# The expert stage of a fused attention, MLP and top-1 MoE kernel: arms in another order, part of a second layer inside them, conversions split, written order outside

## The chip, the cores and the metric

The kernel runs on one core of a Trainium2 chip (trn2). The metric is the device time of one execution in microseconds (us). TensorE does the matrix products, VectorE and ScalarE read their results and convert weights, GpSimd gathers and scatters rows by index, and SyncE (SP) issues the loads of weights.

## The reference, cut to what matters

```
attn_out = chunked attention(q, k, v, mem_k, mem_v)   # 2 x 8 heads x 768 x 64
x = tokens of attn_out                                # 1536 x 512
h = x @ w_in;  x = (h * sigmoid(1.702 * h)) @ w_out   # 512 -> 2048 -> 512
logits = x @ w_gate                                   # 8 experts
expert_idx = argmax(logits);  gate_w = its softmax probability
for each expert e: disp[e] = the tokens that chose it (at most 384)
    h = max(disp[e] @ w1[e], 0)                       # 512 -> 1024
    y = h @ w2[e]                                     # 1024 -> 512
out[token] = gate_w * y[its expert, its place]
```

The change lies in the last part, the eight experts. With the inputs that are timed, the experts get 224, 291, 128, 160, 256, 160, 189 and 128 tokens, in the order in which the kernel works them (`EORDER`). The text calls them expert 0 to expert 7 in that order.

## The kernel before, in words

All products are made in float32 from two parts: each operand is split into a high part (rounded to the matmul's type) and a low part (what is left), and three products are summed: high x high, high x low, low x high. So a weight matrix has to be converted before use. A `Piece` is a quarter of `w1` or `w2` of an expert (512 KB): `Piece.hi` (L292) writes the high part on ScalarE (L295), `Piece.lo` (L297) the low part on VectorE (L300). Each expert has eight pieces, four of `w1` and four of `w2`. They come over SP's queue (L241) into eight raw buffers; a raw buffer is free for the next load when the low part has been taken. `w_next(e, keep)` (L347) converts the next piece, both halves one behind the other, unless it is numbered `keep` or more among the pieces of expert e+1; `steps(part)` (L1027) does so until `KEEPS[part]` is reached. Six weight slots of half a matrix hold what is converted: the four of the expert at work and two more.

Tokens are worked in blocks of 128, gathered by GpSimd (L827), transposed by TensorE (`trans`, L843) and split into `xs`. Expert 0 has its first block done in the stage before and goes through `after_first` (L1162). The others go through `others` (L1186). How many blocks an expert has is known only on the chip, so `others` branches on the count in a register (`tc.If`), and each engine runs one of three arms:

- lone (at most 128 tokens; `one`, L1140, `first_of`, L1035): the first layer with the tokens as the stationary operand (`block_h`, L951, matmuls L964), its relu (L968), transposes back (`turn`, L973, L977, L978), all instructions in written order;
- narrow (129 to 192; `narrow_two`, L1144, `first_of_narrow`, L1059): eight chunks `fc` of the first layer for 192 columns (L1080, L1082, four `psh` buffers of PSUM), each read by ScalarE and VectorE into `low` (L1085, L1086) and split by `scale` (L1068, L1069), with the 64 columns of the second block packed by GpSimd into `hp` (L1071); then the second block's second layer `small2(1)` (L939);
- wide (over 192; `wide_two`, L1149, `first_of_two`, L1047): eight chunks for 256 columns (L879, L882, L883), the second layer of block 1 (L1004), and a nested branch for a third block (`third`, L1130).

In every arm w_next is called at some chunks (`PUMPS`, `PUMPS1`), the next expert's two blocks are transposed (`next_trans`, L1022), and `steps(0)` ends what the arm may convert: `KEEPS[0] = 4`, that is all four pieces of the next `w1`. Behind the arms the engines meet again (the join): the slots of `w1` are freed, the first block's whole second layer follows (`layer2_part(0, ...)`, L998, L1004: eight chunks of three matmuls), `steps(1)` converts the next `w2`, a second branch sends the second block (`send_second`: VectorE's L945 and L946 for a narrow one, ScalarE's L1009 for a wide one), and block 0 is sent.

The Tile framework puts instructions of one level in an order of its own by priority and readiness, unless dependencies are added by hand. `in_order` (L140) adds them along each engine; `turned` (L1043) does so for ScalarE and VectorE alone. Outside the arms nothing fixes the order of TensorE, ScalarE and VectorE. The pieces are counted at build time, so every arm has to convert the same pieces (`both`, L1097).

Of the kernel before, what the change touches and what calls it, by code (L numbers as in the profile page):

```python
# [21 lines left out]
P = 128  # L22
# [10 lines left out]
FROM = 150  # L33
EV1 = 2
PUMPS = (1, 3, 5)
PUMPS_N = (1, 3, 5)
RAWS = 4
RT = (4, 7)
LOADS = 1000
AHEAD = 4  # L40
EARLY = 12
KEEP = 4
KEEPS = (4, 8, 8)
HALF = P // 2
PUMPS1 = (0, 1, 1, 0)
GFC = 2
EORDER = (1, 2, 0, 3, 5, 6, 7, 4)
KNOWN = 8
TFC = 5
STEPS = (2, 4, 2, 5, 4)  # L50
TAIL1 = 8
DEPTH = 2
# [40 lines left out]
def kernel(  # L93
# [45 lines left out]
    @contextmanager  # L139
    def in_order(only=None):  # L140

        traced = nc.cur_bb.bb.instructions
        n0 = len(traced)
        yield
        last = {}
        for i in traced[n0:]:
            if only is not None and i.engine not in only:
                continue
            if i.engine in last:
                tc.add_manual_dep(  # L150
                    i, last[i.engine], mybir.DependencyInfo(mybir.DependencyClass.NoSync, mybir.DependencyReason.DATA),
                    reason="in_order")
            last[i.engine] = i.name


    const = ctx.enter_context(tc.tile_pool(name="const", bufs=1, side="left"))
    wp = ctx.enter_context(tc.tile_pool(name="wp", bufs=1, side="left"))
# [189 lines left out]
    def w_next(e, keep=KEEP):  # L347

        name, i = (flight[0].name, flight[0].i) if flight else pieces[min(w_at[0], w_end[0] - 1)][:2]
        if not flight or name[1] * 8 + 4 * (name[0] == "w2") + 2 * name[2] + i >= 8 * e + 8 + keep:  # L350
            return False
        w_step()
        w_loads(8 * F // 512)
        return True

    def w_state():
        return w_at[0], list(flight), list(free_slots), list(free_raw), dict(where), set(ready)
# [9 lines left out]
    def w_loads(n):  # L367
        while len(flight) < n and w_load():
            pass
# [446 lines left out]
    def expert_parts(e, ep, tp, cnt):  # L816
# [205 lines left out]
        def next_trans():  # L1022
            if e + 1 < E:
                parts[e + 1].trans(0)
                parts[e + 1].trans(1)

        def steps(part):  # L1027
            while w_next(e, KEEPS[part]):
                pass
# [5 lines left out]
        def first_of(b):  # L1035

            with in_order():
                turn = block_h(b, pump_one)
                next_trans()
                turn()  # L1040
                steps(0)

        def turned():  # L1043

            return in_order(only=(mybir.EngineType.Activation, mybir.EngineType.DVE))

        def first_of_two():  # L1047

            with turned():
                for fc in range(F2):  # L1050
                    mm, act = layer1(fc)
                    if fc in PUMPS:
                        w_next(e, KEEPS[0])
                    if fc == TFC:
                        with tc.issue_after(mm):
                            next_trans()
                steps(0)

        def first_of_narrow():  # L1059

            t, _ = xs_of(0)
            h = hT_of(0)
            n = P + HALF
            lows = {}

            def scale(fc):
                low = lows.pop(fc)
                nc.scalar.activation(out=h[:, 0, fc, :n], in_=low, func=AF.Relu)  # L1068
                nc.vector.scalar_tensor_tensor(out=h[:, 1, fc, :n], in0=low, scalar=0.0, in1=h[:, 0, fc, :n].bitcast(F32),  # L1069
                                               op0=ALU.max, op1=ALU.subtract)  # L1070
                nc.gpsimd.tensor_copy(hT["pair"][:, fc], h[:, :, fc, P:n])  # L1071

            with turned():
                for fc in range(F2):
                    w_tile(("w1", e, fc // 4), 0)
                    w = w_tile(("w1", e, fc // 4), 1)
                    f0 = (fc % 4) * P
                    ps = psum("h", "psh")
                    for c in range(KC):
                        nc.tensor.matmul(ps[:, :2 * n].rearrange("p (z n) -> p z n", z=2), lhsT=w[:, 0, c, f0:f0 + P],  # L1080
                                         rhs=t[:, :, c, :n], start=c == 0, stop=False)
                        mm = nc.tensor.matmul(ps[:, :2 * P], lhsT=w[:, 1, c, f0:f0 + P], rhs=t[:, 0, c, :],  # L1082
                                              start=False, stop=c == KC - 1)
                    low = lows[fc] = ep.tile([P, 512], F32, tag="hs", name="low", bufs=2)[:, :n]
                    nc.scalar.activation(out=low, in_=ps[:, n:2 * n], func=AF.Copy)  # L1085
                    nc.vector.tensor_tensor(out=low, in0=ps[:, :n], in1=low, op=ALU.add)  # L1086
                    if fc > 0:
                        scale(fc - 1)
                    if fc in PUMPS_N:
                        w_next(e, KEEPS[0])  # L1090
                    if fc == TFC:
                        with tc.issue_after(mm.ins):
                            next_trans()
                scale(F2 - 1)
                steps(0)

        def both(cond, yes, no):  # L1097

# [38 lines left out]
            with tc.If(cnt[ex] > b * P):  # L1137
                both(cnt[ex] > b * P + HALF, lambda: go(True), lambda: go(False))

        def one():  # L1140

            first_of(0)

        def narrow_two():  # L1144

            first_of_narrow()
            small2(1)

        def wide_two():  # L1149

            first_of_two()
            layer2_part(1, y_of(1), range(F2))
            third(2)

        def send_second(wide):
# [30 lines left out]
        def others():  # L1186

            assert NCB == 3
            for b in range(2):
                y_of(b)  # L1190
                gate(b)
            for b in range(2, NCB):
                load(b)
                hT_of(b)
                xs_of(b)
            both(cnt[ex] < P + 1, one, lambda: both(cnt[ex] < P + HALF + 1, narrow_two, wide_two))
            w1_done()
            layer2_part(0, y_of(0), range(F2))
            with turned():
                steps(1)  # L1200
            with tc.If(cnt[ex] > P):
                both(cnt[ex] > P + HALF, lambda: send_second(True), lambda: send_second(False))
            send(0)

        return SimpleNamespace(adopt=adopt, load=load, trans=trans, xs_of=xs_of, after_first=after_first, others=others,
# [195 lines left out]
    with ExitStack() as st:  # L1401
# [23 lines left out]
        with tc.high_priority(offset=LOADS):  # L1425
            w_loads(8 * (F // 512))
        not_before.clear()
        for e in range(E):
            if e + 1 < E:
                for b in range(2):  # L1430
                    parts[e + 1].load(b)
                parts[e + 1].xs_of(0)
            if e == 0:
                with tc.high_priority(offset=LOADS):
                    w_loads(8 * (F // 512))
                first_block.send()
                nc.gpsimd.tensor_tensor(out=pair, in0=ident[:, :HALF], in1=ident[:, HALF:], op=ALU.add)
                parts[0].after_first()
            else:
                parts[e].before_arms()  # L1440
                with tc.high_priority(offset=LOADS):
                    w_loads(8 * (F // 512))
                parts[e].others()
            for j in range(F // 512):
                w_free(("w2", e, j))


# [68 lines left out]
```

## Time and profile before

| what | us |
|---|---|
| median of three runs | 556.79 |
| lowest, highest | 552.14, 556.85 |
| profiled execution | 552.85 |
| its span, first to last instruction | 551.0 |

The profiled execution's own time is 552.85 us, of which 551.0 us is the span that the profile shows. Times in rows are microseconds from the span's start; "ns" stands for the mean of one instruction in a group. In the timeline a row is: start, length, engine, line, operation, output <- input, shape, count, and in brackets the idle time of the engine just before it and what ended it. PEld is TensorE's weight load. [...]

### The profile page before, as it was taken

Reading aid. Unit: us, or ns where it says so; the run is one execution under the profiler, and the core shown is the slowest. Engines: PE = TensorE matmul, PEld = TensorE weight load, DVE = VectorE, ACT = ScalarE, POOL = GpSimd, SP = SyncE. Lnnn points to the kernel's source line nnn. Section 1 sums busy time; section 2 is a strip of 40 time slices with the busy share of each in tenths; the row PEclk is TensorE's granted clock in tenths of the full one; section 3 lists DMA queues with packets and bytes.
Section 4 is the critical chain, followed back from the end, with each engine's and each line's share of the span. In section 5 each row is a group of like instructions: output and inputs, shape, how many; then the busy total and the mean of one; then the engine's idle time right before and its main releaser. Section 6 shows DMA issues by size and latency. Waiting matters only on the chain. (4 is left out here: it accounts for less than half of the span.)

```text
span 551.0 us, 10686 instructions
## 1 busy us (share of the span) xinstructions
PE 511.2 (93%) x4081; PEld 435.7 (79%) x4085; DVE 317.8 (58%) x637; ACT 277.8 (50%) x577; POOL 124.7 (23%) x131
## 2 busy tenths in 40 slices
PE   8799999999999999999999999999969689979674
PEld 3589889899999999999888887788849488949453
DVE  4999893678952742232474446384484838484710
ACT  2898977756642532222553344574293636455520
POOL 3335433334200120000000001530344322222200
PEclk9999999999999999999999999999999999979797
DMA  8887563142430031000484114993489566653100
GB/s 325 290 315 272 198 212 104 34 146 95 157 106 1 2 113 40 1 1 0 132 269 137 40 59 122 319 348 114 163 278 339 155 218 196 233 172 133 28 26 20
DMA packets 39158, 81.48 MB, mean 148 GB/s; under 512 B 3945, under 2 KB 10089, under 8 KB 39082
## 3 DMA queue, kind: packets, MB, share of 16 engines
q1 hardware_dynamic: 36010, 70.66, 37.8%
q0 software_dynamic: 3072, 9.80, 5.6%
q8 instruction: 48, 0.79, 0.6%
q14 instruction: 28, 0.23, 0.2%
HBM read 70.96 MB, written 9.75 MB: 146 GB/s over the span
## 5 line engine op out<-in xcount | busy, mean ns | idle before, releaser
L547 PEld LDWEIGHTS psh<-xT,w 128*128 128x128 f32 x1152 | 147.0, 188 | 7.9 <-ACT g L566 0.3
L590 PE MATMUL acc<-w,g 128*128 128x512 f32 x576 | 153.0, 400 | 0.0
L547 PE MATMUL psh<-xT,w 128*128 128x256 f32 x1152 | 151.6, 280 | 0.0
L590 PEld LDWEIGHTS acc<-w,g 128*128 128x128 f32 x576 | 100.7, 188 | 19.5 <-issue 2.1
L562 ACT ACTIVATE sg<-psh 128x256 f32<-128x256 f32 x96 | 36.7, 383 | 126.0 <-PE psh L547 125.6
L300 DVE TENSOR_TENSOR w<-raw,w 128x1024 fp32r<-128x1024 f32 x64 | 76.0, 1221 | 21.6 <-ACT w L295 15.5
L570 DVE TENSOR_TENSOR g<-sg,g 128x256 fp32r<-128x256 f32 x78 | 38.2, 490 | 80.3 <-ACT g L566 77.7
L1004 PE MATMUL psy<-w,hT 128*128 128x512 f32 x240 | 67.3, 439 | 16.6 <-ACT w L295 12.3
L1004 PEld LDWEIGHTS psy<-w,hT 128*128 128x128 f32 x240 | 50.2, 214 | 32.4 <-ACT w L295 14.4
L295 ACT ACTIVATE w<-raw 128x1024 fp32r<-128x1024 f32 x64 | 64.8, 1054 | 10.6 <-DMA raw<-in_w_dram 9.2
L827 POOL DMA_INDIRECT xr<-rows,taker x23 | 29.9, 1300 | 31.2 <-PE psy L1004 11.7
L566 ACT ACTIVATE g<-psh 128x256 fp32r<-128x256 f32 x96 | 36.3, 379 | 0.0
L601 DVE SCALAR_TENSOR_TENSOR x<-acc,x 128x512 f32<-128x512 f32 x36 | 24.1, 686 | 20.8 <-PE acc L590 20.8
L725 POOL DMA_INDIRECT y<-rows,taker x1 | 1.2, 1222 | 123.8 <-DVE cnt_i L732 123.8
L1080 PE MATMUL psh<-xs,w 128*128 128x384 f32 x96 | 28.5, 338 | 0.0
L1009 ACT ACTIVATE y<-psy,gt 128x512 f32<-128x512 f32 x10 | 6.7, 684 | 43.1 <-PE psy L1004 43.1
L1082 PE MATMUL psh<-xs,w 128*128 128x256 f32 x96 | 26.9, 280 | 0.0
L879 PE MATMUL psh<-xs,w 128*128 128x256 f32 x192 | 24.0, 284 | 2.5 <-issue 1.6
L300 POOL TENSOR_TENSOR w<-w,w 128x512 fp32r<-128x512 f32 x12 | 16.5, 1382 | 41.6 <-ACT w L295 41.4
L879 PEld LDWEIGHTS psh<-xs,w 128*128 128x128 f32 x192 | 23.3, 189 | 3.3 <-issue 1.8
L290 POOL TENSOR_TENSOR w<-w,rest 128x512 int32<-128x512 int32 x13 | 17.4, 1338 | 36.9 <-DVE w L276 33.5
L265 ACT ACTIVATE w<-raw 128x512 f32<-128x512 f32 x32 | 21.3, 674 | 8.7 <-DMA raw<-in_w_out_dram 6.7
(163 smaller groups left out, 671.6 us busy)
## 6 DMA issues: line engine op xcount, KB each, us to landing
raw<-in_w_dram SPq DMA_DIRECT2D x64, 512.0 KB, 4.9
raw<-in_w_out_dram SPq DMA_DIRECT2D x16, 512.0 KB, 3.6
raw<-in_w_in_dram SPq DMA_DIRECT2D x16, 512.0 KB, 6.3
vt<-in_v_dram SPq DMA_DIRECT2D x12, 512.0 KB, 5.3
kt<-in_k_dram SPq DMA_DIRECT2D x12, 368.0 KB, 5.2
qt<-in_q_dram SPq DMA_DIRECT2D x12, 256.0 KB, 5.1
out_dram<-blank SPq DMA_DIRECT2D x12, 256.0 KB, 2.6
rows<-x SPq DMA_DIRECT2D x5, 520.0 KB
```

Source lines behind the costliest of these rows:

```text
L295: nc.scalar.activation(out=w_dst(self.name, self.i, 0), in_=w, func=AF.Copy)
L300: eng.tensor_tensor(out=lo, in0=w, in1=hi.bitcast(F32), op=ALU.subtract)
L547: nc.tensor.matmul(ps, lhsT=w[:, wz, c, i * P:(i + 1) * P], rhs=xT[tb][:, xz, c, :], start=n == 0, stop=n == 3 * KC - 1)
L562: nc.scalar.activation(out=sg_t[u], in_=h_t[u], func=AF.Silu, scale=1.702)
L566: g_last[:1] = [nc.scalar.activation(out=g[:, 0], in_=h_t.pop(u), func=AF.Silu, scale=1.702).ins]
L570: lo = eng.tensor_tensor(out=g[:, 1], in0=sg_t.pop(u), in1=g[:, 0].bitcast(F32), op=ALU.subtract)
L590: nc.tensor.matmul(acc_t[tb][s], lhsT=g[:, gz, s * P:(s + 1) * P], rhs=w[:, wz, wi, :], start=i == 0 and n == 0, stop=u == last_of(k, tb) ...
L827: return nc.gpsimd.indirect_dma_start(out=t, out_offset=None, in_=rows[:, :], in_offset=bass.IndirectOffsetOnAxis(ap=taker[:, b, ex:ex + 1 ...
L879: mm = nc.tensor.matmul(ps, lhsT=w[:, wz, c, f0:f0 + P], rhs=t[:, xz, c, :], start=m == 0, stop=m == 3 * KC - 1)
L1004: nc.tensor.matmul(ps, lhsT=h[:, hz, fc, o:o + P], rhs=w[:, wz, fc % 4, :], start=fc == 0 and n == 0, stop=fc == F2 - 1 and n == 2)
L1080: nc.tensor.matmul(ps[:, :2 * n].rearrange("p (z n) -> p z n", z=2), lhsT=w[:, 0, c, f0:f0 + P], rhs=t[:, :, c, :n], start=c == 0, stop=False)
L1082: mm = nc.tensor.matmul(ps[:, :2 * P], lhsT=w[:, 1, c, f0:f0 + P], rhs=t[:, 0, c, :], start=False, stop=c == KC - 1)
```

## The change

The order of the three arms in the code becomes narrow, wide, lone (one condition is turned round). The first three chunks of the first block's second layer (`HEAD2 = 3`, nine matmuls) go into the arms (`head`, in the lone arm two before the last turn and one after it); the other five (`tail`) come behind the join, and now behind `steps(1)` and the second branch. The arms convert three pieces of the next `w1` and no longer four; `begin` does a piece's high half, and `end`, a chunk later, its low half and the next load. The transposes of the next expert move from the arms to just behind the join. `turned` fixes TensorE's order too. In the narrow arm a tile holds two `low` parts, so that four can be open. And `as_written` adds order dependencies along TensorE, ScalarE and VectorE for everything outside the arms, with a branch counted as an instruction of all three. Expert 0 keeps `first_of` and `w_next`.

```diff
@@ constants @@
-PUMPS_N = (1, 3, 5)
-KEEPS = (4, 8, 8)
+KEEPS = (3, 8, 8)
+HEAD2 = 3
-TFC = 5
@@ -153,6 +152,23 @@
             last[i.engine] = i.name
 
 
+    @contextmanager
+    def as_written():
+
+        traced = nc.cur_bb.bb.instructions
+        n0 = len(traced)
+        yield
+        engines = (mybir.EngineType.PE, mybir.EngineType.Activation, mybir.EngineType.DVE)
+        last = {}
+        for i in traced[n0:]:
+            arms = type(i).__name__ == "BassTileConditionalBlock"
+            mine = engines if arms else (i.engine,) if i.engine in engines else ()
+            for name in {last[x] for x in mine if x in last}:
+                tc.add_manual_dep(
+                    i, name, mybir.DependencyInfo(mybir.DependencyClass.NoSync, mybir.DependencyReason.DATA),
+                    reason="as_written")
+            last.update({x: i.name for x in mine})
+
     const = ctx.enter_context(tc.tile_pool(name="const", bufs=1, side="left"))
     wp = ctx.enter_context(tc.tile_pool(name="wp", bufs=1, side="left"))
     dram = ctx.enter_context(tc.tile_pool(name="dram", bufs=1, space=DRAM))
@@ -352,6 +368,23 @@
         w_step()
         w_loads(8 * F // 512)
         return True
+
+    def w_apart(e, keep=KEEP):
+
+        if not flight or not w_slot(flight[0].name):
+            return None
+        name, i = flight[0].name, flight[0].i
+        if name[1] * 8 + 4 * (name[0] == "w2") + 2 * name[2] + i >= 8 * e + 8 + keep:
+            return None
+        piece = flight.pop(0)
+        piece.hi()
+
+        def then():
+            piece.lo(nc.vector)
+            free_raw.append(piece.raw)
+            w_loads(8 * F // 512)
+
+        return then
 
     def w_state():
         return w_at[0], list(flight), list(free_slots), list(free_raw), dict(where), set(ready)
@@ -1042,19 +1075,55 @@
 
         def turned():
 
-            return in_order(only=(mybir.EngineType.Activation, mybir.EngineType.DVE))
+            return in_order(only=(mybir.EngineType.PE, mybir.EngineType.Activation, mybir.EngineType.DVE))
+
+        begun = []
+
+        def begin():
+
+            then = w_apart(e, KEEPS[0])
+            if then is not None:
+                begun.append(then)
+
+        def end():
+
+            if begun:
+                begun.pop(0)()
+
+        def head(b):
+
+            layer2_part(b, y_of(b), range(HEAD2))
+
+        def tail(b):
+
+            layer2_part(b, y_of(b), range(HEAD2, F2))
+
+        def first_of_one():
+
+            def pump(i):
+                if i < 2:
+                    begin()
+                if i > 1:
+                    end()
+
+            with in_order():
+                turn = block_h(0, pump)
+                begin()
+                layer2_part(0, y_of(0), range(HEAD2 - 1))
+                turn()
+                end()
+                layer2_part(0, y_of(0), range(HEAD2 - 1, HEAD2))
 
         def first_of_two():
 
             with turned():
                 for fc in range(F2):
-                    mm, act = layer1(fc)
+                    layer1(fc)
+                    end()
                     if fc in PUMPS:
-                        w_next(e, KEEPS[0])
-                    if fc == TFC:
-                        with tc.issue_after(mm):
-                            next_trans()
-                steps(0)
+                        begin()
+                head(0)
+                layer2_part(1, y_of(1), range(F2))
 
         def first_of_narrow():
 
@@ -1079,20 +1148,21 @@
                     for c in range(KC):
                         nc.tensor.matmul(ps[:, :2 * n].rearrange("p (z n) -> p z n", z=2), lhsT=w[:, 0, c, f0:f0 + P],
                                          rhs=t[:, :, c, :n], start=c == 0, stop=False)
-                        mm = nc.tensor.matmul(ps[:, :2 * P], lhsT=w[:, 1, c, f0:f0 + P], rhs=t[:, 0, c, :],
-                                              start=False, stop=c == KC - 1)
-                    low = lows[fc] = ep.tile([P, 512], F32, tag="hs", name="low", bufs=2)[:, :n]
+                        nc.tensor.matmul(ps[:, :2 * P], lhsT=w[:, 1, c, f0:f0 + P], rhs=t[:, 0, c, :],
+                                         start=False, stop=c == KC - 1)
+                    if fc % 2 == 0:
+                        two = ep.tile([P, 512], F32, tag="hs", name="low", bufs=2)
+                    low = lows[fc] = two[:, fc % 2 * 2 * P:][:, :n]
                     nc.scalar.activation(out=low, in_=ps[:, n:2 * n], func=AF.Copy)
                     nc.vector.tensor_tensor(out=low, in0=ps[:, :n], in1=low, op=ALU.add)
                     if fc > 0:
                         scale(fc - 1)
-                    if fc in PUMPS_N:
-                        w_next(e, KEEPS[0])
-                    if fc == TFC:
-                        with tc.issue_after(mm.ins):
-                            next_trans()
+                    end()
+                    if fc in PUMPS:
+                        begin()
                 scale(F2 - 1)
-                steps(0)
+                head(0)
+                small2(1)
 
         def both(cond, yes, no):
 
@@ -1137,19 +1207,9 @@
             with tc.If(cnt[ex] > b * P):
                 both(cnt[ex] > b * P + HALF, lambda: go(True), lambda: go(False))
 
-        def one():
-
-            first_of(0)
-
-        def narrow_two():
-
-            first_of_narrow()
-            small2(1)
-
         def wide_two():
 
             first_of_two()
-            layer2_part(1, y_of(1), range(F2))
             third(2)
 
         def send_second(wide):
@@ -1193,13 +1253,13 @@
                 load(b)
                 hT_of(b)
                 xs_of(b)
-            both(cnt[ex] < P + 1, one, lambda: both(cnt[ex] < P + HALF + 1, narrow_two, wide_two))
+            both(cnt[ex] > P, lambda: both(cnt[ex] < P + HALF + 1, first_of_narrow, wide_two), first_of_one)
             w1_done()
-            layer2_part(0, y_of(0), range(F2))
-            with turned():
-                steps(1)
+            next_trans()
+            steps(1)
             with tc.If(cnt[ex] > P):
                 both(cnt[ex] > P + HALF, lambda: send_second(True), lambda: send_second(False))
+            tail(0)
             send(0)
 
         return SimpleNamespace(adopt=adopt, load=load, trans=trans, xs_of=xs_of, after_first=after_first, others=others,
@@ -1425,24 +1485,25 @@
-        for e in range(E):
+        with as_written():
+            for e in range(E):
...
```

`first_of_one`, `first_of_two` and `first_of_narrow` are whole functions of an arm now; `one` and `narrow_two` are gone.

## Rows read from the trace of the kernel before

**Rows 1.** The page, busy time, share of the span, instructions: TensorE.
```profile
PE 511.2 (93%) x4081; PEld 435.7 (79%) x4085; DVE 317.8 (58%) x637; ACT 277.8 (50%) x577; POOL 124.7 (23%) x131
```

**Rows 2.** Busy time in stretches, one for each of experts 2 to 7.
```profile
core 0: us, PE busy (x) PEld busy (x) DVE busy (x) ACT busy (x) POOL busy (x), PEclk, DMA share, GB/s
398.82:418.92 20.10, 14.80 (x65) 11.85 (x64) 14.55 (x20) 13.38 (x23) 9.14 (x6) 0.92 0.91 315
418.92:445.44 26.52, 21.91 (x114) 18.46 (x113) 17.53 (x32) 14.07 (x31) 8.69 (x13) 0.94 0.70 224
445.44:471.20 25.76, 24.04 (x154) 21.34 (x153) 14.50 (x22) 13.50 (x24) 5.64 (x5) 1.00 0.66 213
471.20:498.10 26.90, 22.95 (x114) 19.10 (x113) 17.71 (x32) 14.06 (x31) 7.14 (x11) 0.87 0.61 197
498.10:524.92 26.82, 22.23 (x113) 18.55 (x112) 17.63 (x34) 14.37 (x33) 6.51 (x11) 0.87 0.16 52
524.92:544.62 19.70, 15.20 (x57) 11.06 (x55) 1.39 (x2) 3.08 (x5) 1.01 (x1) 0.83 0.04 16
```

**Rows 3.** Waits of TensorE, 349 to 545: total us, times, longest.
```profile
PE psy L1004 <- ACT w L295: 12.3, 4, 5.3
PE psy L939 <- POOL hp L1071: 6.0, 6, 1.7
...
PE psu L973 <- ACT hs L968: 0.7, 1, 0.7
```

**Rows 4.** Timeline of TensorE in expert 3 (narrow).
```profile
425.85 1.04 PE L846 MATMUL pst<-ident,xr 128*128 128x128 f32 x8
429.03 2.51 PE L939 MATMUL psy<-w,hp 128*128 128x512 f32 x10
433.22 0.73 PE L939 MATMUL psy<-w,hp 128*128 128x512 f32 x2 [1.68 <-POOL hp L1071]
...
438.18 7.42 PE L1004 MATMUL psy<-w,hT 128*128 128x512 f32 x24 [2.58 <-ACT w L295]
```

**Rows 5.** Timeline of ScalarE and VectorE in expert 3.
```profile
430.99 1.28 DVE L851 TENSOR_TENSOR xs<-pst,xs 128x512 fp32r<-128x512 f32 x2
...
432.90 0.33 ACT L1085 ACTIVATE low<-psh 128x192 f32<-128x192 f32 x1 [1.64 <-DVE hT L1069]
...
435.00 5.77 DVE L300 TENSOR_TENSOR w<-raw,w 128x1024 fp32r<-128x1024 f32 x5 [0.55 <-ACT w L295]
440.80 0.76 DVE L945 TENSOR_SCALAR y<-psy,gt 64x512 f32<-64x512 f32 x1
```

**Rows 6.** Timeline at the joins of experts 2 and 7 (lone).
```profile
408.23 6.89 DVE L300 TENSOR_TENSOR w<-raw,w 128x1024 fp32r<-128x1024 f32 x6
...
411.75 7.34 PE L1004 MATMUL psy<-w,hT 128*128 128x512 f32 x24 [5.30 <-ACT w L295]
...
535.22 2.07 PE L1004 MATMUL psy<-w,hT 128*128 128x512 f32 x4 [2.79 <-issue]
538.32 6.30 PE L1004 MATMUL psy<-w,hT 128*128 128x512 f32 x20 [1.03 <-issue]
```

**Rows 7.** DMA from 532.4 to 535.3: busy tenths in 40 slices, the only queue.
```profile
DMA  0008000000000000000000000000000000000000
...
q8 instruction: 1, 0.02, 2.2%
```

**Rows 8.** Timeline of TensorE in experts 0, 1 and 4.
```profile
352.93 0.18 PE L1016 MATMUL psy<-ones 128*32 128x8 bf16 x1
...
357.19 5.98 PE L1004 MATMUL psy<-w,hT 128*128 128x512 f32 x23
...
384.95 4.00 PE L939 MATMUL psy<-w,hT 128*128 128x512 f32 x16
...
449.43 6.59 PE L879 MATMUL psh<-xs,w 128*128 128x256 f32 x53 [1.57 <-issue]
```

**Rows 9.** Groups by line: VectorE's two steps per narrow chunk; busy, mean ns.
```profile
L1069 DVE SCALAR_TENSOR_TENSOR hT<-low,hT 128x192 fp32r<-128x192 f32 x24 | 8.7, 363 | 0.5 <-ACT hT L1068 0.5
...
L1086 DVE TENSOR_TENSOR low<-psh,low 128x192 f32<-128x192 f32 x24 | 8.5, 355 | 7.2 <-ACT low L1085 6.2 <-issue 1.0
```

More of the change, by code (lines that the diff above doesn't have):

```diff
@@ L1427 @@
         not_before.clear()
-        for e in range(E):
[L1429 to L1445, printed above, removed]
+        with as_written():
+            for e in range(E):
+                if e + 1 < E:
+                    for b in range(2):
+                        parts[e + 1].load(b)
+                    parts[e + 1].xs_of(0)
+                if e == 0:
+                    with tc.high_priority(offset=LOADS):
+                        w_loads(8 * (F // 512))
+                    first_block.send()
+                    nc.gpsimd.tensor_tensor(out=pair, in0=ident[:, :HALF], in1=ident[:, HALF:], op=ALU.add)
+                    parts[0].after_first()
+                else:
+                    parts[e].before_arms()
+                    with tc.high_priority(offset=LOADS):
+                        w_loads(8 * (F // 512))
+                    parts[e].others()
+                for j in range(F // 512):
+                    w_free(("w2", e, j))
 _OUTS = [((1536, 512), 'float32')]
```

## The prediction

> **What bounds the kernel now.** I read the page first: TensorE is busy for 93% of the span [rows 1], so only the places where it stands still, or runs at half clock, have something to give. The diff touches the expert stage alone, so next I cut that stage by expert with busy time in stretches. Experts 2, 3, 5, 6 and 7 in the order worked hold 20.1, 26.5, 26.9, 26.8 and 19.7 us, with TensorE busy for 14.8, 21.9, 23.0, 22.2 and 15.2 us of it and a mean granted clock of 0.92 to 0.83; wide expert 4 is busy 24.0 of 25.8 us at clock 1.00 [rows 2]. So narrow and lone experts lose time and wide ones hardly do. The view of waits, TensorE alone, says where: 12.3 us in four waits of `psy` (L1004), the first block's second layer behind the join, put down to ScalarE's weight halves; 6.0 us of L939 on the packed halves `hp` from GpSimd; 0.7 us of L973, a lone block's last turn, on the relu before it [rows 3].
>
> The timeline of expert 3 (narrow) shows the pattern. The first layer's eight chunks run from 418.92 to about 429.1, with the next expert's transposes inside (425.85); then L939 does ten matmuls and waits 1.68 us, and after the arm L1004 waits 2.58 us [rows 4]. Behind them is the eviction queue. The transposes' two low halves hold VectorE from 430.99 for 1.28 us; ScalarE's `low` at 432.90 waited 1.64 us for VectorE's L1069 (two `low` buffers, so chunk fc needs fc-2 gone); the arm's last piece starts its low half on VectorE only at 435.00, first of five that take 5.77 us (1.15 each) [rows 5]. It ends near 436.2; TensorE starts at 438.18.
>
> Lone experts show the same without the packing. In expert 2 L1004 starts 5.30 us after its last predecessor, at 411.75, while VectorE has six low halves in a row from 408.23; in expert 7, which has no pieces left to convert, it still waits 2.79 us on "issue", then 1.03 us more after four matmuls [rows 6]. In the first of these waits the only transfer is one packet of code (queue 8, 0.02 MB); it lies in the fourth of forty slices of 0.0725 us, so it begins at about 532.65, and TensorE starts 2.5 us later [rows 6, 7]. So two things are late behind an arm: the arm's own ScalarE/VectorE tail, and code.
>
> After such a wait matmuls are slow: 24 of L1004 take 7.34 us at 411.75 and 7.42 at 438.18 [rows 4, 6]; 23 of the same shape take 5.98 at full clock (0.26 each, 6.24 for 24) [rows 8]. That is the half clock of the mean in rows 2.
>
> **The change part by part.** All sums are against the profiled execution, 552.85 us (span 551.0 and 1.85 around it). The median of the three runs, 556.79, lies 3.94 above it; I add that at the end.
>
> *Narrow arm, transposes out, fourth piece out, four `low` halves, halves a chunk apart.* The TensorE path: first layer 9.2 us (418.92 to 425.85 is six chunks, 1.155 each [rows 2, 4]); nine matmuls of the head 9 x 0.26 = 2.3; sixteen of L939 4.0 [rows 8]; behind the join eight transposes 1.0 [rows 4]; fifteen of the tail 3.9. Sum 20.4 us, to which gaps come. The head puts 2.3 us between the first layer and L939, and the evictions no longer wait behind 1.28 us of transposes, so I cost the wait for `hp` at nothing.
>
> But VectorE now has a cycle of its own, since written order puts the transposes' low halves ahead of the five conversions. Behind the join: 1.28 + 5.77 us [rows 5], the narrow block's two `y` steps 0.76 and about the same again [rows 5], 1.5. In the arm: eight times 0.355 + 0.363 us [rows 9] is 5.7, and three low halves of 1.15 make 9.2. Together 17.8 us. From the arm's last eviction to the next transposes' low half VectorE idles: packing and the last two matmuls, some 0.8 us; the join, 2.5 us if code has to come (532.65 to 535.22 [rows 6, 7]); transposes 1.0; ScalarE's high half, some 0.5 by the low half's 0.64. That is 4.8 us, and 0.7 (an estimate) for gates and branches: 23.3 us a narrow expert. VectorE's cycle is longer than TensorE's 20.4 plus a gap of 1, so I take it. From 26.52, 26.90 and 26.82 this gives 3.2 + 3.6 + 3.5 = **10.3 us**. Bounds: 21.4 us each if the cycle is slack (16 us gained), 25.7 if both branches behind the arm are bare (3 us gained).
>
> *Lone arm.* Two chunks of the second layer (six matmuls, 1.6 us) stand before the last turn and one after it. Expert 2: 5.30 us of wait and 7.34 - 6.24 = 1.1 of slow clock go; what is late next is VectorE's low half of the last turn and the third piece's, then the branch: about 1.4 us behind the transposes. So 5.0 us. Expert 7: 2.79 + 1.03 + (2.07 + 6.30 - 6.24) = 5.95 [rows 6], and 0.7 of waiting for the relu [rows 3], which the two chunks cover, go; 1.4 comes back: 5.2 us. Together **10.2 us** (bounds: 5, with a bare code load of 2.8 and slow clock left; 11.5, nothing left).
>
> *Wide arms (experts 1 and 4).* They ended at the join and had next to no gap. Now they leave over the lone arm, and their transposes, branch and tail stand behind it. No row shows a wide arm that leaves by a jump. From below: the 1.57 us of "issue" inside expert 4's arm [rows 8] goes with the shorter way in, a gain of 1.6. From above: a bare code load at the exit and at the branch, 2.5 us each. TensorE has 24 matmuls queued ahead of the exit, which speaks for the lower half: **+1 us** each.
>
> *The second block's branch, now ahead of the tail.* Only eight transposes (1.0 us) stand between join and branch; where it stood among L1004, four matmuls were too few (1.03 us bare) [rows 6]. Bounds 0 to 2.5 us; about 1 is inside the figures above.
>
> *Expert 0 in written order.* Its skip matmul ran at 352.93 with no idle time in front of it [rows 8], behind first-layer matmuls that the scheduler had drawn ahead of the branch. Now the branch comes first, with only the previous stage's matmuls queued: 0 to 2.5 us, I take **+1**. Its third-block test also moves ahead of L1004, inside that bound.
>
> *Moved with no price.* The fourth piece of each next first layer goes from arm to join: ScalarE's and VectorE's steps are counted, and its load on SP, which waits for that low half, is issued some microseconds later; the eight raw buffers hold an expert's worth. If that cover fails it is one late piece at the next fourth chunk, about 1 us. GpSimd's queue keeps its gathers and gains nothing. The end of the kernel behind the last matmul is unchanged.
>
> Sum: -10.3 - 10.2 + 2 + 1 = -17.5 us; 552.85 - 17.5 = 535.35; with 3.94, **539.3 us**.
>
> [...] A code packet stands in the wait behind expert 7's arm [rows 7], while the skip at 352.93 was reached over a whole block left out, without a gap [rows 8]. [...]
>
> **The rivals.**
> *Short jumps free.* The wide exit and the branch ahead of the tail cost nothing, and so does expert 0's. It decides if every branch target but the far joins is at hand. For it: the skip without a gap [rows 8]. Against: 1.03 us after four matmuls [rows 6]. Worked out: wide and expert 0 give back the 3, the two lone gaps 2, the narrow ones 0.5 each: -24, 533 us.
>
> *VectorE's queue behind the join becomes the bound.* All conversions now wait for the transposes, and loads wait for them. It decides once the next arm's first eviction starts later than four chunks (4.6 us, four `psh` buffers) after the arm's first matmul. For it: VectorE busy 17.5 to 17.7 of 26.5 to 26.9 us already [rows 2], 8.5 us of it now behind the transposes. Against: wide arms evict little. A further 3 us on each narrow expert, 1 on each of four others: -17.5 + 13 = -4.5, 552 us.
>
> *Every branch bare (the other side).* Two branches stand close behind each arm, and if both load code, 2.5 us each less 1 us of cover, TensorE idles 4 us at every join and the half clock follows (1.1 us as in expert 2). Narrow experts are then 20.4 + 4 + 1.3 = 25.7 (-3 in all), lone ones gain 2 each, wide ones lose 5 each, expert 0 2.5, expert 7's end 0.5 more: +6, 563 us. It decides from about 3.5 us idle per join. For it: the waits and the packet of expert 7 [rows 6, 7]. Against: the queues ahead of arms' ends are full once the waits are gone.
>
> *The change doesn't do what it says*: the head waits for the arm's last eviction after all and nothing moves, 557 us.
>
> **How the numbers follow.** Forecast 0.52, with its own range 532 to 548; short jumps free 0.14; VectorE's queue 0.20; every branch bare 0.11; no effect 0.03. A measurement of this kernel tells about 1%, 5.6 us, from no change. Faster by more than that: 0.52 + 0.14 + 0.05 of the VectorE case = 0.71. Slower: 0.11 and a little of expert 0's bound, 0.12. The rest, 0.17, is within. The range is 530 to 555: it leaves out the branch case above and the bottom end of the free-jump case.
>
> **What would show it.** Right: L1004's wait on ScalarE's weight halves and L939's on `hp` gone, narrow experts near 23 us, lone ones near 15, clock near 1.00 in their stretches. The VectorE step is right if first evictions in a narrow arm start 4 to 6 us behind its first matmul. Wrong: 2 to 3 us of "issue" before the transposes or the tail in every expert, or half clock still behind each join; then the branches, not the tails of the arms, were the price. If wide experts do not grow, the free-jump reading holds.

## The result, and the profile after

The changed kernel takes 536.25 us (median of 4 runs, 535.17 to 538.89) against 556.82 us of the kernel before beside it: ratio 0.9659, 95% interval 0.9604 to 0.9713. The forecast was 539.3. The gain is 20.6 us by the medians and 17.6 us by the span of the profiled executions (551.0 to 533.4 us); 17.5 us were forecast.

The cut by expert, after, answers to [rows 2]; the columns are the same: busy time and instructions of each engine, then the mean granted TensorE clock (1.00 is full speed), the share of the DMA engines and GB/s. The rows are experts 0 to 7 in order, all eight.

```profile
351.06:365.49 14.43, 13.44 (x66) 10.94 (x66) 8.87 (x12) 10.97 (x17) 6.73 (x5) 1.00 1.00 346
365.49:400.09 34.60, 33.67 (x205) 29.47 (x204) 15.99 (x29) 13.91 (x29) 5.18 (x5) 1.00 0.50 169
400.09:413.98 13.89, 13.11 (x65) 10.53 (x65) 11.92 (x17) 12.35 (x21) 4.20 (x3) 1.00 0.89 279
413.98:438.75 24.77, 20.22 (x114) 17.71 (x112) 16.66 (x31) 14.34 (x32) 13.73 (x15) 1.00 0.78 283
438.75:463.82 25.07, 23.99 (x153) 21.27 (x152) 15.23 (x25) 12.36 (x24) 5.91 (x5) 1.00 0.65 215
463.82:489.35 25.53, 20.42 (x113) 17.62 (x112) 15.83 (x31) 14.62 (x33) 7.18 (x12) 1.00 0.65 207
489.35:514.62 25.27, 21.70 (x113) 19.01 (x112) 17.72 (x33) 14.65 (x33) 7.34 (x11) 0.93 0.38 131
514.62:526.99 12.37, 12.37 (x56) 9.64 (x56) 6.92 (x12) 5.06 (x11) 1.93 (x2) 1.00 0.11 34
```

The same cut of the kernel before has two more rows, experts 0 and 1 (the first begins at expert 0's first matmul; the stage in front ended at 349.27):

```profile
349.10:364.15 15.05, 13.85 (x67) 10.41 (x65) 9.48 (x12) 11.78 (x18) 5.74 (x5) 1.00 1.03 347
364.15:398.82 34.67, 33.74 (x205) 29.58 (x205) 17.62 (x31) 14.45 (x30) 8.46 (x5) 1.00 0.53 181
```

Lone experts (2 and 7) gained 6.2 and 7.3 us, narrow ones (3, 5, 6) 1.75, 1.4 and 1.55, wide ones (1 and 4) 0.1 and 0.7, expert 0 about 0.5: 19.5 us in all. The span fell by 17.6: the stage in front, which the diff leaves alone, ended 1.8 us later in this execution (351.06 against 349.27), and the granted clock between 10 and 30 us was 0.91 there against 1.00.

TensorE's waits in the expert stage, after (total, times, longest), answer to [rows 3]:

```profile
PE pst L879 <- issue: 7.3, 3, 3.6
PE psh L1149 <- DVE low L1157: 3.9, 3, 1.8
PE psy L972 <- POOL hp L1140: 1.8, 1, 1.8
PE psh L912 <- DVE hT L916: 0.9, 1, 0.9
```

Lines have moved: L879 is the transposes (before L846), L1037 the second layer (L1004), L972 the narrow second block (L939), L1149 and L912 the first layers of the narrow and the wide arm (L1080, L879), L1157 and L916 VectorE's steps (L1086, L883), L997 and L1006 the lone arm's first layer and last turn (L964, L973). The 12.3 us put down to weight halves are gone, and of 6.0 us for `hp` 1.8 are left. In their place stand three waits of issue (the engine waited for nothing that the profile shows) in front of the transposes, all behind narrow arms, and three at the fifth chunk of a narrow first layer, for VectorE. By the timeline the three of issue are 3.58, 2.20 and 1.47 us in experts 3, 5 and 6.

The timeline of expert 3, TensorE and VectorE, answers to [rows 4, 5]:

```profile
419.32 0.62 DVE L1157 TENSOR_TENSOR low<-psh,low 128x192 f32<-128x192 f32 x2
419.73 0.44 PE L1149 MATMUL psh<-xs,w 128*128 128x384 f32 x1 [0.97 <-DVE low L1157]
426.81 3.89 PE L972 MATMUL psy<-w,hp 128*128 128x512 f32 x16
428.73 0.40 DVE L1138 SCALAR_TENSOR_TENSOR hT<-low,hT 128x192 fp32r<-128x192 f32 x1 [0.17 <-ACT hT L1137]
434.28 1.06 PE L879 MATMUL pst<-ident,xr 128*128 128x128 f32 x8 [3.58 <-issue]
435.57 1.29 DVE L884 TENSOR_TENSOR xs<-pst,xs 128x512 fp32r<-128x512 f32 x2 [6.44 <-ACT xs L883]
```

The sixteen matmuls of L972 run without a stop. VectorE has its last eviction done at 429.13, then idles 6.44 us for the transposes, which wait for TensorE's way to the join. VectorE is late at the start of a narrow arm too: here, behind a lone arm, its first eviction began at 419.32, 5.3 us behind the arm's first matmul (413.98), and the fifth chunk waited 0.97 us. Behind a wide arm (expert 5) it was 5.5 us late, behind a narrow one (expert 6) 6.2, and the fifth chunk waited 1.10 and 1.80 us. In the stretch from 431 to 436 us five packets of the instruction queues, that is of code, pass:

```profile
q8 instruction: 2, 0.03, 3.1%
q14 instruction: 3, 0.02, 1.4%
```

Expert 7, in contrast to [rows 6], goes through its join without a gap: eighteen matmuls follow the last turn, three of them in the arm and fifteen behind it, at full clock.

```profile
522.21 0.60 PE L1006 MATMUL psu<-ident,hs 128*128 128x128 f32 x4
522.57 4.42 PE L1037 MATMUL psy<-w,hT 128*128 128x512 f32 x18
```

### The profile page after: what moved, and what is told of

It reads as the page before. It is cut to its first block, busy times and chain, and to the rows that moved or that the text cites. A ratio compares the mean times of both kernels' runs of the same rounds, so it can differ in the third digit from the quotient of the medians.

```text
span 533.4 us, 10652 instructions
## 1 busy us (share of the span) xinstructions
PE 503.1 (94%) x4085; PEld 432.2 (81%) x4085; DVE 315.4 (59%) x637; ACT 277.3 (52%) x577; POOL 124.9 (23%) x131
## 5 line engine op out<-in xcount | busy, mean ns | idle before, releaser
L623 PEld LDWEIGHTS acc<-w,g 128*128 128x128 f32 x576 | 100.6, 188 | 19.5 <-issue 2.1
L1037 PE MATMUL psy<-w,hT 128*128 128x512 f32 x240 | 59.7, 398 | 0.3
L1037 PEld LDWEIGHTS psy<-w,hT 128*128 128x128 f32 x240 | 43.9, 188 | 10.5 <-issue 0.9
L1149 PE MATMUL psh<-xs,w 128*128 128x384 f32 x96 | 30.3, 354 | 3.9 <-DVE low L1157 3.9
L860 POOL DMA_INDIRECT xr<-rows,taker x23 | 28.6, 1245 | 12.6 <-issue 6.1
L884 DVE TENSOR_TENSOR xs<-pst,xs 128x512 fp32r<-128x512 f32 x14 | 9.0, 685 | 34.6 <-ACT xs L883 34.6
L883 ACT ACTIVATE xs<-pst 128x512 fp32r<-128x512 f32 x14 | 7.6, 596 | 38.8 <-PE pst L879 38.8
L1151 PE MATMUL psh<-xs,w 128*128 128x256 f32 x96 | 27.8, 289 | 0.0
L1043 POOL DMA_INDIRECT out_dram<-y,taker x10 | 14.2, 1422 | 52.7 <-ACT y L1042 22.9
L281 ACT ACTIVATE w<-raw 128x512 f32<-128x512 f32 x32 | 21.3, 675 | 9.7 <-DMA raw<-in_w_out_dram 7.5
```

The costliest lines, as they stand in the source:

```text
L623: nc.tensor.matmul(acc_t[tb][s], lhsT=g[:, gz, s * P:(s + 1) * P], rhs=w[:, wz, wi, :], start=i == 0 and n == 0, stop=u == last_of(k, tb) ...
L860: return nc.gpsimd.indirect_dma_start(out=t, out_offset=None, in_=rows[:, :], in_offset=bass.IndirectOffsetOnAxis(ap=taker[:, b, ex:ex + 1 ...
L1037: nc.tensor.matmul(ps, lhsT=h[:, hz, fc, o:o + P], rhs=w[:, wz, fc % 4, :], start=fc == 0 and n == 0, stop=fc == F2 - 1 and n == 2)
```

## The experiments

There are twelve kernels in three groups of four, each group with the kernel before beside it. The kernel before had a median of 555.21 us beside the first group (lone first, narrow last, no written order, one chunk), 554.25 beside the second (only the order, transposes in the arms with and without written order, halves together) and 556.61 beside the third (the other four). The second group ran on another chip than the first and third, so kernels of different groups, and the result above, are compared by their ratios to the kernel before; 0.01 is about 5.5 us.

**Arms in the order of before** (lone, narrow, wide), all else as changed.

```diff
-both(cnt[ex] > P, lambda: both(cnt[ex] < P + HALF + 1, first_of_narrow, wide_two), first_of_one)
+both(cnt[ex] < P + 1, first_of_one, lambda: both(cnt[ex] < P + HALF + 1, first_of_narrow, wide_two))
```

> The arms in the order of before (lone, narrow, wide), all else as changed. Theory 'code': an arm that leaves over other arms' code waits for a load at the join, one that runs on into the join does not. Then the two lone experts wait 2 to 3 us of issue at their joins again, with half clock behind, the narrow ones keep the 3.6, 2.2 and 1.5 us that they have in the changed kernel, the wide ones stay as they are: 4 to 7 us more than the changed kernel, 540 to 543 us. Rival 'cover': the lone waits went because three chunks of the second layer lie in the arm; the order of the arms is indifferent, within 1 us of 536.

542.36 us (ratio 0.9754, 0.9678 to 0.9831; the change 0.9659), 5 to 6 us more than the change. TensorE's timeline behind the lone arms of experts 2 and 7:

```profile
411.43 1.48 PE L879 MATMUL pst<-ident,xr 128*128 128x128 f32 x8 [2.74 <-issue]
...
530.89 5.30 PE L1037 MATMUL psy<-w,hT 128*128 128x512 f32 x15 [1.88 <-issue]
```

Both waits are back, 2.7 and 1.9 us, though three chunks stand in the arm; fifteen matmuls take 5.30 us, 0.35 each against 0.25 above. Narrow joins kept theirs (2.25, 3.7, 2.3). So it is the order of the code and not the cover.

**Only the order, in the kernel before.**

```diff
-both(cnt[ex] < P + 1, one, lambda: both(cnt[ex] < P + HALF + 1, narrow_two, wide_two))
+both(cnt[ex] > P, lambda: both(cnt[ex] < P + HALF + 1, narrow_two, wide_two), one)
```

> The kernel before with nothing but the order of the arms changed to narrow, wide, lone. Theory 'code': the lone experts run on into the join, so expert 7 loses its 2.8 and 1.0 us of issue and the half clock behind (5 to 6 us), expert 2 little, since it waits there for VectorE's conversions; narrow and wide ones stay: 5 to 7 us faster than before in the same call, some 548 against 555. Rival 'cover': without the second layer's chunks in the arm the waits stay, and the time is within 2 us of before.

543.95 us, ratio 0.9828 (0.9783 to 0.9873): 10.3 us from one turned condition, more than either theory gave. Expert 2 took 13.1 us and expert 7 13.1, against 20.1 and 19.7 [rows 2]. Expert 2's timeline says that its 5.30 us in [rows 6] were not due to ScalarE's or VectorE's late work:

```profile
409.02 5.78 PE L1004 MATMUL psy<-w,hT 128*128 128x512 f32 x24
...
410.44 0.68 DVE L978 TENSOR_TENSOR hT<-psu,hT 128x512 fp32r<-128x512 f32 x1
411.04 2.35 DVE L300 TENSOR_TENSOR w<-raw,w 128x1024 fp32r<-128x1024 f32 x2
```

TensorE starts L1004 at 409.02, ahead of VectorE's half of the last turn and of the arm's last conversions (ScalarE's begin at 409.87), which the view of waits had named. Narrow experts stayed at 27.5 to 28.4 us with L939 and L1004 waiting 7.2 and 7.1 us in all; TensorE waited 3.2 us on the way into expert 2's arm, which now lies far off; wide expert 4 fell to 23.9 us.

**Narrow arm last** (wide, lone, narrow), all else as changed.

```diff
-both(cnt[ex] > P, lambda: both(cnt[ex] < P + HALF + 1, first_of_narrow, wide_two), first_of_one)
+both(cnt[ex] > P + HALF, wide_two, lambda: both(cnt[ex] < P + 1, first_of_one, first_of_narrow))
```

> Arms in the order wide, lone, narrow, all else as changed. Theory 'code': the narrow experts' waits before the transposes (7.3 us in the changed kernel) fall to under 1.5 us together, the lone ones, which now leave over the narrow arm, get 0 to 3 us each, the wide ones stay hidden by the 24 matmuls in front of their exit: between 6 us faster and no change, 530 to 536. Rival 'tail': the wait is for the arm's end on the other engines, so the 7.3 us stay whatever the order, and the time is 536 to 540.

538.95 us (ratio 0.9679, 0.9587 to 0.9771; the change 0.9659), no gain. TensorE's waits, the longest and the next:

```profile
PE psh L1149 <- issue: 8.3, 1, 8.3
PE psh L1149 <- DVE low L1157: 2.7, 2, 1.7
```

No transposes wait any more, as the code theory has it; but on the way into expert 3's narrow arm TensorE stood 8.3 us, from 415.22 to 423.52. Experts 5 and 6 were entered over the same arms with waits of at most 0.3 us. The same order in the kernel that has the transposes back in the arms and no written order (529.7 us, below; its lines lie two further down, so that L1151 and L1153 are the two matmuls of a narrow first layer):

> The same kernel with its arms in the order wide, lone, narrow. Theory 'code': no wait at the narrow joins, little at the lone ones behind 2.7 us of queued work, and a long way into the narrow arm, where the same order cost 8.3 us of issue in expert 3 of the other kernel while loads of weights filled the queues: if that wait is the order's, the time is 531 to 536; rival 'chance': that wait was one late packet, it does not come again, and the time is 524 to 528.

543.41 us (ratio 0.9764, 0.9708 to 0.9821), against a ratio of 0.9560 with the order of the change. On its three ways into that arm TensorE stood 8.9, 1.1 and 5.6 us, and in expert 5 another 3.4 us behind the first eight matmuls, so the wait came again with the order:

```profile
PE psh L1151 <- issue: 19.1, 4, 8.9
...
422.86 0.66 PE L1151 MATMUL psh<-xs,w 128*128 128x384 f32 x1 [8.95 <-issue]
469.44 0.42 PE L1151 MATMUL psh<-xs,w 128*128 128x384 f32 x1 [1.11 <-issue]
474.29 0.45 PE L1151 MATMUL psh<-xs,w 128*128 128x384 f32 x1 [3.43 <-issue]
500.21 0.66 PE L1151 MATMUL psh<-xs,w 128*128 128x384 f32 x1 [5.64 <-issue]
```

**No written order**, all else as changed.

```diff
-        with as_written():
+        if True:
```

> Written order outside the arms taken away, all else as changed. Theory: written order costs as much as it gives, since it holds VectorE's conversions behind the transposes (the 3.9 us of L1149 waiting for VectorE at the fifth chunk) and orders tail and branch; without it those 3.9 us shrink and others appear, 533 to 539 us. Rival: written order carries the gain; waits of the first block's second layer on weight halves come back, 541 us or more.

555.23 us (ratio 0.9950, 0.9898 to 1.0002): nearly all of the gain gone. TensorE's waits:

```profile
PE pst L879 <- DMA xr<-rows,taker: 12.6, 4, 3.8
PE psh L997 <- issue: 7.4, 3, 3.1
PE pst L879 <- DVE xs L884: 6.2, 2, 3.6
```

And GpSimd and TensorE at the way from expert 1 into expert 2:

```profile
401.61 1.00 POOL L860 DMA_INDIRECT xr<-rows,taker x1 [0.30 <-ACT y L1042]
...
403.37 0.60 PE L879 MATMUL pst<-ident,xr 128*128 128x128 f32 x4
407.13 0.63 PE L879 MATMUL pst<-ident,xr 128*128 128x128 f32 x4 [3.16 <-DMA xr<-rows,taker]
410.88 6.29 PE L997 MATMUL psh<-w,xs 128*128 128x512 f32 x18 [3.12 <-issue]
```

Three blocks of four matmuls are transposed here (399.44, 403.37, 407.13), around the last fifteen matmuls of expert 1 and ahead of expert 2's arm, where the change has two; twelve such matmuls ran already at 363.57 and 367.19, ahead of expert 1's arm, where the change has none. So transposes are drawn in front of the next arms, and the last four wait for a gather issued some 5 us before. TensorE stands 3.16 us for the gather, then, with nothing queued, 3.12 us on the way into the arm.

**Transposes back in the arms**, with and without written order.

```diff
             w1_done()
-            next_trans()
             steps(1)
...
 # narrow and wide arm
                 head(0)
+                next_trans()
...
 # lone arm
                 layer2_part(0, y_of(0), range(HEAD2 - 1))
+                next_trans()
                 turn()
```

> The changed kernel with the next expert's transposes back in the arms, behind the three chunks of the second layer (narrow and wide) or before the last turn (lone). Theory 'VectorE cycle': VectorE takes the transposes' low halves while TensorE still has the second block's second layer, and starts the five conversions without waiting through the join, so the waits at the fifth chunk (3.9 us of L1149 and 0.9 of L912) and the 1.8 us of hp go; the narrow joins keep their code load of 2 to 3.5 us each: 3 to 7 us less than the changed kernel, 529 to 533. Rival: the joins' waits grow by what the transposes no longer fill and the time stays within 2 us of 536.

530.3 us (ratio 0.9581, 0.9537 to 0.9625), against 0.9659 for the change 4 us less by the ratios and 6 by the medians. The waits for VectorE in a first layer (3.9 us at the narrow fifth chunks, 0.9 in a wide arm) fell to 0.8 us, those for `hp` to none; behind the narrow arms 3.3, 1.3 and 1.5 us stand at the tail.

```profile
PE psy L1037 <- ACTq L1173: 3.3, 1, 3.3
...
PE psh L1151 <- DVE low L1159: 0.8, 1, 0.8
```

> As the kernel with the transposes back in the arms, and without written order outside them. Theory 'drawn ahead': written order matters because, without it, transposes that stand outside the arms are drawn ahead of the next expert's arms, where their gather has not landed; with the transposes inside nothing can be drawn, so written order is worth under 3 us here. Rival 'tail': it matters for where the second branch and the tail stand too, and the loss is again 8 us or more.

529.71 us (ratio 0.9560, 0.9522 to 0.9597), the fastest of all: written order is worth nothing here. Narrow experts took 27.0, 21.3 and 23.4 us, lone ones 13.1 and 12.3:

```profile
412.97:439.98 27.01, 21.64 (x113) 18.84 (x111) 21.01 (x39) 16.37 (x38) 12.09 (x15) 0.94 0.87 295
...
463.95:485.21 21.26, 19.98 (x113) 17.85 (x112) 16.76 (x31) 14.40 (x31) 7.70 (x10) 1.00 0.74 220
485.21:508.64 23.43, 20.11 (x114) 17.25 (x112) 18.47 (x34) 15.03 (x32) 8.99 (x12) 1.00 0.25 87
```

The first of them, expert 3, is no shorter than before: VectorE comes late into it (2.5 us of wait at its fifth chunk).

**The arms' own parts.** One chunk in place of three, in the changed kernel and in the 529.7 us kernel:

```diff
-HEAD2 = 3
+HEAD2 = 1
```

> One chunk of the second layer in the arms in place of three, all else as changed. Theory 'cover': the lone arms have nothing behind the last turn, so TensorE waits there for VectorE's low half and the join, 1.5 to 2.5 us each with half clock behind expert 7's, and the narrow ones wait up to 1.6 us each longer for hp: 4 to 9 us more, 540 to 545. Rival 'order alone': the three chunks hide nothing that the order of arms had not freed, within 1.5 us of 536.

538.39 us (ratio 0.9691, 0.9616 to 0.9766; the change 0.9659), some 2 us more, which can't be told apart from none. The lone arms have no wait behind the turn with one chunk either; `hp` waits rise from 1.8 to 4.8 us, and the narrow ways out took 5.3, 0.7 and 2.0 us:

```profile
433.76 1.94 PE L879 MATMUL pst<-ident,xr 128*128 128x128 f32 x8 [5.28 <-issue]
```

> The same kernel with one chunk of the second layer in the arms in place of three. Theory: the chunks stand between the first layer and the second block's second layer and hide the last evictions and the packing; without two of them the narrow experts wait up to 1.6 us each for hp and the joins stay: 2 to 6 us more, 532 to 536. Rival: the waits merely change place with the tail behind the join, within 1 us of 530.

534.85 us (ratio 0.9593, 0.9540 to 0.9646; with three chunks 0.9560, 0.9522 to 0.9597): 5 us more by the medians, 2 by the ratios, which is not settled. In the profile the waits at the narrow tails are 3.2, 3.0 and 1.8 us in place of 1.6, 1.3 and 1.9, and expert 0, whose code is the same, holds 1.7 us more.

Two open `low` halves in place of four, in the 529.7 us kernel:

```diff
-                    if fc % 2 == 0:
-                        two = ep.tile([P, 512], F32, tag="hs", name="low", bufs=2)
-                    low = lows[fc] = two[:, fc % 2 * 2 * P:][:, :n]
+                    low = lows[fc] = ep.tile([P, 512], F32, tag="hs", name="low", bufs=2)[:, :n]
```

> The same kernel with two low parts in a narrow arm in place of four, nothing else. Theory: ScalarE's low waits for VectorE's second step two chunks back whenever a piece's low half lies between (1.2 us, three per arm), the packed halves come later and L939's successor waits for hp 1 to 3 us per narrow expert: 533 to 538. Rival: with transposes and the fourth piece out of the way two are enough, within 1 us of 530.

537.27 us (ratio 0.9651, 0.9604 to 0.9698; with four 0.9560): 5 us more by the ratios, 7.6 by the medians. Not by `hp`, which no matmul waits for: the waits at the narrow tails grew from 1.6, 1.3 and 1.9 us to 1.9, 2.0 and 3.8 (the third of two parts each), that on the way into expert 4 from 1.2 to 2.4, and the mean granted clock fell from 0.992 to 0.985. The size was right; the place was not.

Halves of a piece together, in the changed kernel:

```diff
             if then is not None:
-                begun.append(then)
+                then()
```

> The changed kernel with a piece's low half straight behind its high half. Theory: VectorE waits half a microsecond for each high half (0.55 us, three per arm), 1 to 1.7 us later per narrow expert where VectorE sets the pace, less in the others: 2 to 5 us more, 538 to 541. Rival: VectorE has slack there and the time is within 1 us of 536.

538.25 us (ratio 0.9712, 0.9673 to 0.9751; the change 0.9659), 2 to 3 us more, the same span in the profile (533.5): too small to settle.

**Wide arm first** (wide, narrow, lone), in the 529.7 us kernel.

```diff
-both(cnt[ex] > P, lambda: both(cnt[ex] < P + HALF + 1, first_of_narrow, wide_two), first_of_one)
+both(cnt[ex] > P, lambda: both(cnt[ex] > P + HALF, wide_two, first_of_narrow), first_of_one)
```

> The kernel with transposes in the arms and no written order outside (529.7 us), its arms in the order wide, narrow, lone. Theory 'code, by distance': a narrow arm now leaves over the lone arm alone and its joins (1.6, 1.3 and about 1.4 us there) fall to under 0.5 each; a wide one leaves over two arms but has 24 matmuls in front; the way into the narrow arm gets long and is covered by fifteen matmuls in front: 2 to 5 us less, 525 to 528. Rival: every way out that jumps costs the same, and the long way in adds a wait of 1 to 3 us: 529 to 534.

532.59 us (ratio 0.9567, 0.9521 to 0.9614; with the order of the change 0.9560), no difference by the ratios. The narrow joins lost their waits as the distance theory has it, and the ways into the narrow arms of experts 3, 5 and 6 cost as much: 1.7, 0.9 and 3.1 us at the first matmul (the first and third put down to VectorE), and 4.1 of issue behind the first few of expert 3. Neither theory alone; this order only moves the price.

```profile
PE psh L1153 <- issue: 4.1, 1, 4.1
PE psh L1151 <- DVE y L979: 3.1, 1, 3.1
...
PE psh L1151 <- DVE w L316: 1.7, 1, 1.7
```

## Why the prediction was right, and where its steps were not

The sum held (17.5 us forecast, 17.6 in the span), in part by luck: its terms missed in opposite directions, and the expert stage itself gave 19.5 us, of which the stage in front took 1.8 back.

*Lone arms: 10.2 forecast, 13.5 measured.* The step that failed is "what is late next is VectorE's low half of the last turn". Nothing is late next. I had taken the releaser's name in the view of waits for the cause. The order alone brings the two experts to 13.1 us each, with all conversions still in place; the chunks in the arm add the little to 12.4 in expert 7. What ended was the way out by a jump.

*Narrow arms: 10.3 forecast, 4.7 measured.* TensorE's busy time came out (20.4 forecast; 20.2, 20.4 and, with the granted clock at 0.50 from 497.41 to 500.82 us, 21.7). VectorE's lateness is real: the forecast wanted first evictions 4 to 6 us behind the first matmul (measured 5.3, 5.5 and 6.2), and the fifth chunk is where TensorE waits for it (3.9 us in three). The mis-sized term is the join. VectorE's idle time through it was 4.8 us in the working and 6.44 in expert 3, where the 3.58 us before the transposes had been costed at 2.5. What failed with it is the choice of the longer of two paths, VectorE's cycle or TensorE's with a gap of 1: the waits add up on TensorE, 7.3 us at the joins, 3.9 at the fifth chunks and 1.8 for `hp`, which had been costed at nothing. That is 13.0 of the 13.2 us by which the three stretches exceed TensorE's busy time. Taking VectorE out of the join's wait, the transposes in the arm, gained 4 to 6 us.

*Wide arms: +2 forecast, -0.8 measured; the second branch 1, measured 0; expert 0 +1, measured about -0.5.* "Every branch bare" fell: transposes and tail follow each other without a gap (459.47 and 460.26 in expert 4). The wide arm leaves over the lone one free, with no idle time ahead of those transposes; whether its 24 queued matmuls or the short distance did that stays open, since it left free over two arms too (narrow last, wide first). Of the rival "short jumps free" two parts came true, the wide exit and the branch ahead of the tail; expert 0's skip has at most the 0.8 us in front of it, put down to ScalarE's `y`. Its 533 us did not, since the far exits of the narrow arms stayed dear.

*The half clock* came back once: 0.93 is the mean of expert 6, with that stretch at 0.50, and 1.00 that of all others after, where five of six rows stood at 0.83 to 0.94 before (the prediction's 0.92 to 0.83 leaves out expert 3's 0.94); in expert 2 before, the granted clock was 0.50 from 411.75 to 414.75 us, behind the wait of 5.30. That is in the lone experts' surplus too.

By the runs the change is three changes. The order of arms gives 10 us alone in the kernel before; taken out of the changed kernel it costs only 5 to 6. The rest of the arms' changes gives some 14 more (543.95 to 529.71 us); of its parts the chunks and the split halves are worth some 2 to 3 us each, not told apart from none, and the four open `low` halves 5 to 8 us in the 529.7 us kernel. The fourth piece behind the join and the second branch ahead of the tail were not tried alone. Moving the transposes behind the join takes 4 to 6 back, and some 22 to 26 without written order, which repairs what that move does and is worth nothing where the transposes stay in the arms.

What stays open is why the long way into the narrow arm takes 8.3 and 8.9 us in expert 3, in both kernels that have the narrow arm last. In these two stretches the DMA engines are busy for 0.98 and 0.96 of the time, and one and two code packets pass. That loads of weights delay code is a guess that no run tried, and in the kernel before 2.79 us were waited with a single code packet under way [rows 6, 7].

## What to carry to other kernels

Of the four orders tried here, the two with the lone arm last, which has little work queued at its end and there runs on into the join, did best (narrow last came level with the change once): turning one condition was worth 10.3 us in the kernel before. A releaser named in a wait is a guess, tested by whether the waiting work starts before that releaser once the order of code has changed. Work that is moved out of a branch comes under the scheduler's hand again, and TensorE paid where it was drawn ahead of its data (12.6 us in four waits for gathers, without written order); moving it back was cheaper than fixing the order.

## What the runs showed of the hardware that was not expected

The way into an arm over others cost more in some experts than the way out, and neither had a fixed price: TensorE waited 0.7 to 5.3 us at narrow arms' exits over another arm or two, and from at most 0.3 up to 8.9 us on the way into a narrow arm that lay behind all others, though fifteen matmuls (3.7 us) ran just ahead of the wait of 8.3 us. Narrow arms that were left over the lone one alone (wide, narrow, lone) had no wait. A skip over one block's code was not always free either: at the test for expert 0's third block, where TensorE has no wait after the change, it waited 1.1 us with the lone arm first, 2.0 with the narrow arm last and 0.8 with one chunk, put down to its own sequencer.
